# Fused attention and gated FFN on one core: remainder weights as 128-partition loads, narrower first gate/up tiles, and a later place for V

## The chip, the cores and the metric

One Trainium2 chip, one of its cores. The metric is device time in microseconds (us) of one launch. The kernel before took 590.39 us (median of 3 runs, 590.12 to 590.76). A ratio is the mean time of one kernel's runs over that of the other's runs of the same rounds, so it isn't quite the ratio of the medians that stand beside it. Intervals are 95%.

In the profile PE is TensorE, PEld its weight loads, DVE VectorE, ACT ScalarE, POOL GpSimd, SP SyncE. A `q` after an engine's name marks its sequencer, which issues DMAs. A "load" is a DMA from memory to on-chip SBUF.

## The reference, cut to what matters

```python
B, S, D, F = 1, 2048, 576, 4608      # bf16; 32 heads of 18; causal window of 256
xn = layernorm(x)
q, k, v = split(xn @ wqkv)
s = softmax_windowed(q @ k.T * 18**-0.5) @ v @ wo
g = silu((sigmoid(xn @ w_gate) * (xn @ w_up)) @ w_down)
return x + s * g
```

All matrix products contract over D = 576 = 4 x 128 + 64 (or over F = 36 x 128). The 64 rows left over are the *remainder* of a weight matrix.

## The kernel before

TensorE works in pairs of 64-row matmuls: one on partitions 0 to 63, one on 64 to 127, side by side. A gate/up tile is 9 such pairs per 512 tokens. Eight pairs take the wide part of the weights (512 rows on 128 partitions). One pair takes the remainder: gate's 64 rows on the lower partitions, up's on the upper.

```python
ROWS = (slice(0, 64), slice(64, 128))

def pair(eng, outs, lhs, rhs, start, stop, swap=0):        # every matmul comes from here
    for i in range(2):
        t = i ^ swap
        res = eng.matmul(outs[i], lhs(ROWS[t], i), rhs(ROWS[t], i), ..., tile_position=(64 * t, 0))
```

Wide parts come in as one load each. Remainders come in as two loads of 64 partitions each:

```python
def load_nat(self, dst, src, ...):
    return self.dma(dst, src[RD:D, :].rearrange("(k p) c -> p k c", p=P), ...)

def load_rem(self, dst, srcs, ...):                        # RD = 64
    return [self.dma(dst[ROWS[t], :], src[0:RD, :], ...) for t, src in enumerate(srcs)]
```

The order of every engine is fixed when the program is built. A planner with its own estimates of durations places the operations, and `o.slack` makes it believe that a load lands later than it would otherwise assume. Gate/up weights come in groups of two tiles: 256 KB of gate, 256 KB of up, and their remainders (`wgr`), the latter for several groups at once. The first three tiles run in two parts of 256 tokens, because the tokens' normalization and transposes come in block by block (128 tokens a block). While nothing real can run, PE multiplies zeros (warm-up) to hold its clock up.

```python
if c == 0 and wg in REM:                                   # REM = {0: (0, 2, 1), 2: (2, 6, 3), 3: (6, 18, 7)}
    f8 = slice(REM[wg][0] * WG * P, REM[wg][1] * WG * P)
    self.op_wgr[wg] = self.load_rem(self.wgr[:, f8], (self.wg[:, f8], self.wu[:, f8]), ...)
...
for part in range(2):                                      # tiles 0 to 2, 256 tokens a part
    los = [gate_up(ft, hs[ft], 0, None if part else hs[ft], part) for ft in range(early)]
    ...
```

The softmax here doesn't subtract the row's maximum and nothing guards it: scores larger than these inputs give would overflow.

Of the kernel before, what the change touches and what calls it, by code (L numbers as in the profile page):

```python
# [5 lines left out]
ALU = mybir.AluOpType  # L6
# [49 lines left out]
NWARM = 110  # L56
NQK = 5
REM = {0: (0, 2, 1), 2: (2, 6, 3), 3: (6, 18, 7)}
# [5 lines left out]
SHARE_NS = 300.0  # L64
DMA_BYTES_PER_NS = 300.0
# [60 lines left out]
class Pool:  # L126
# [11 lines left out]
    def pick(self, n, barred=()):  # L138
        free = []
        for u in self.units:  # L140
            if u in barred:
                continue
            h = self.last[u]
            if h is None:
                free.append((0.0, u))
            elif h.rel and all(r.idx >= 0 for r in h.rel):
                free.append((max(r.end for r in h.rel) + 90.0, u))
        if len(free) < n:
            return None
        free.sort()  # L150
        got = free[:n]
        return max(t for t, _ in got), sorted(u for _, u in got)
# [70 lines left out]
class Builder:  # L223
# [38 lines left out]
    def alloc_memory(self):  # L262
# [21 lines left out]
        self.wgr, _ = seq("wgr", [P, F])  # L284
# [92 lines left out]
    def load_x(self, c, i=0):  # L377
        if c == 0:
            for i in range(BPC):
                t = self.x0[:, i, :]  # L380
                src = self.x[i * P:(i + 1) * P, :]
                if i == BPC - 1:
                    src = src.rearrange("(a p) d -> a p d", a=8)
                self.x_dma[i] = (self.dma(t, src, P * D * 2, f"dma:x{i}", ("x0", i), prio=0), t)
            return
        st = c * BPC + i
        slots, dd = [], []
        for _ in range(2):
            s_, d_ = self.r_xr.produce()
            slots.append(s_)  # L390
            dd += d_
        assert slots[1] == slots[0] + 1
        o = self.dma(self.xr[:, slots[0]:slots[0] + 2, :],
                     self.x[st * P:(st + 2) * P, :].rearrange("(t p) d -> p t d", p=P),
                     2 * P * D * 2, f"dma:x{st}", ("x", slots[0]), deps=[dd, self.hm[6] if c == 1 else None], prio=5)
        o.slack = 5000.0
        for j in range(2):
            self.x_dma[st + j] = (o, self.xr[:, slots[j], :])
# [5 lines left out]
    def load_rem(self, dst, srcs, name, lane, prio, deps=()):  # L404
        return [self.dma(dst[ROWS[t], :], src[0:RD, :], RD * src.shape[1] * 2, name, lane + (t,), deps=deps, prio=prio)
                for t, src in enumerate(srcs)]

    def build_consts(self):
# [24 lines left out]
        self.op_wqk += self.load_rem(self.wqkr[:, :], (wq, wk), "dma:wqkr", ("wqkr",), 5)  # L433
# [3 lines left out]
        self.op_wv += self.load_rem(self.wvr[:, :], (wv[:, 0:288], wv[:, 288:D]), "dma:wvr", ("wvr",), 6)  # L437
# [7 lines left out]
    def build_attn_consts(self):  # L445
        op = self.op
        d = [self.ln_rs]
        vv = self.v_aug[:, 0:NVS * VSZ].rearrange("p (g d) -> p g d", d=VH)
        o = op("POOL", 400, lambda e: e.memset(vv[:, :, DH:VH], 1.0), "init:vones", deps=d, prio=1)
        self.op_vones = o  # L450
        self.op_vzero = o = op("POOL", 100, lambda e: e.memset(self.v_aug[:, NVS * VSZ:NVS * VSZ + VH], 0.0), "init:vzero", deps=[o], prio=1)
        self.op_qz = o = op("POOL", 4300, lambda e: e.memset(self.qk[:, :, :, :], 0.0), "init:qz", deps=[o], prio=1)
        self.op_kz = o = op("POOL", 2200, lambda e: e.memset(self.kprev[:, :, :], 0.0), "init:kz", deps=[o], prio=1)
        lo = slice(0, SW)
        o = op("POOL", 150, lambda e: e.memset(self.mask[lo, :], 1.0), "init:m0", deps=[o], prio=1)
        o = op("POOL", 200, lambda e: e.affine_select(self.mask[lo, 0:SW], self.mask[lo, 0:SW], pattern=[[-1, SW]],
                                                      compare_op=ALU.is_ge, fill=0.0, base=-1, channel_multiplier=1), "init:m1", deps=[o], prio=1)
        o = op("POOL", 200, lambda e: e.affine_select(self.mask[lo, SW:P], self.mask[lo, SW:P], pattern=[[1, SW]],
                                                      compare_op=ALU.is_ge, fill=0.0, base=0, channel_multiplier=-1), "init:m2", deps=[o], prio=1)
        self.op_mask = op("DVE", 200, lambda e: e.tensor_copy(self.mask[SW:P, :], self.mask[lo, :]), "init:m3", deps=[o], prio=1)  # L460
        hs = []
        for q in range(4):
            for t in range(2):
                hs.append(op("DVE", 60, lambda e, q=q, t=t: e.memset(self.half[32 * q:32 * q + 32, t:t + 1], float(q % 2 == t)),
                             f"init:half{q}{t}", deps=d, prio=1))
        self.op_half = hs

    def build_ln(self, c):
# [3 lines left out]
        for i in range(BPC):  # L472
            st = c * BPC + i
            if c and i % 2 == 0:
                self.load_x(c, i)
            pr = 2 if c or i > 1 else 0
# [18 lines left out]
            dup = op("DVE", 180, lambda e, sn=sn: e.tensor_copy(self.xnr[:, sn, 0:RD], self.xnr[:, sn, RD:2 * RD]),  # L495
                     f"ln:dup:{st}", deps=[ap], prio=pr)
            if c:
                self.r_xr.release(i % 2, ap)
            self.r_st.release(ss, ap)
            if c:  # L500
                fl = self.flip(self.xnT[:, xs, :, i * P:(i + 1) * P], self.xnr[:, sn, :], f"flip:x:{st}", ("fx", xs, i),
                               deps=[dup, war], prio=2)
                self.r_xn.release(sn, fl)
                self.op_xnT[c].append(fl)
                continue
            h = self.pool_s.hold()

            def f_tr(eng, h=h, sn=sn):
                return self.transposes(eng, h, lambda r, o: self.xnr[r, sn, o:o + P])
            tr = op("PE", KB * 29.5, f_tr, f"tr:{st}", deps=[dup, self.op_ident, war], prio=pr if c else 0, acq=h)  # L510
            self.r_xn.release(sn, tr)

            def f_xe(eng, h=h, i=i, xs=xs):
                dst = self.xnT[:, xs, :, i * P:(i + 1) * P].rearrange("p k (t c) -> p t k c", t=2)
                if eng is self.nc.scalar:
                    return eng.activation(dst, self.tr_src(h), ACTF.Copy)
                return eng.tensor_copy(dst, self.tr_src(h))
            dve = st == BPC - 1
            xe = op("DVE" if dve else "ACT", dve_ns(KB * P, 1.9) if dve else act_ns(KB * P), f_xe, f"xe:{st}", deps=[tr], prio=pr)
            h.release(xe)  # L520
            self.op_xnT[c].append(xe)

    def transposes(self, eng, h, src):
        res = None
        for k in range(KB):
            for t in range(2):
                o = h.units[0] * 2048 + t * 1024 + k * 64
# [17 lines left out]
    def build_qk(self, c, gi):  # L545
# [25 lines left out]
        for u in range(H):  # L571
# [12 lines left out]
            for w, (dst, src) in enumerate(moves):  # L584
                o = self.dma(dst, src, n_ * 2 * NT * 2 // len(moves), f"dma:sp:{c}:{u}:{w}:{gi}", ("qk", par, gi),
                             deps=[ev, war, self.op_qz], prio=1, eng="POOL")
                self.op_sp.setdefault((c, hg), []).append(o)
# [18 lines left out]
    def build_v(self, c):  # L606
        op = self.op
        xs = c % 2
        for i in range(BPC):
# [6 lines left out]
                               [self.op_xnT[c][i], self.op_wv, war])  # L616
# [16 lines left out]
    def build_attn(self, c, hg):  # L633
# [128 lines left out]
        if (c, hg) == (0, 0):  # L762
            self.op_wo_w = [self.load_nat(self.wo_sb[:, :, :], self.wo, "dma:wo", ("wo",), 8, [pv])]
            self.op_wo_w += self.load_rem(self.wor[:, :], (self.wo[:, 0:288], self.wo[:, 288:D]), "dma:wor", ("wor",), 8, [pv])
# [39 lines left out]
    def build_ffn(self, c):  # L804
# [16 lines left out]
        def weights(wg):  # L821
# [5 lines left out]
            if c == 0 and wg in REM:  # L827
                f8 = slice(REM[wg][0] * WG * P, REM[wg][1] * WG * P)
                self.op_wgr[wg] = self.load_rem(self.wgr[:, f8], (self.wg[:, f8], self.wu[:, f8]), f"dma:wgr:{wg}", ("wgr", wg), REM[wg][2])
            if c == 0:  # L830
                ds += self.op_wgr[0 if wg < 2 else 2 if wg < 6 else 3]
# [13 lines left out]
        def gate_up(ft, h, half, acq, part=None, deps=()):  # L845
            sw, fc = slots[ft // WG], slice((ft % WG) * P, (ft % WG + 1) * P)
            n = NT if part is None else NT // 2
            t0 = n * (part or 0)
            xin = self.op_xnT[c] if part is None else self.op_xnT[c][2 * part:2 * part + 2]

            def lhs(r, t, k):
                return self.wgs[r, sw, k - 1, t, fc] if k else self.wgr[r, ft * P:(ft + 1) * P]

            def f(eng):
                return turn(eng, [bank(h, w)[:, t0:t0 + n] for w in range(2)], lhs, lambda r, t, k: x_in[r, k, t0:t0 + n], half)
# [18 lines left out]
        if early:  # L874
# [3 lines left out]
            for part in range(2):  # L878
                los = [gate_up(ft, hs[ft], 0, None if part else hs[ft], part) for ft in range(early)]
                for ft in range(early):  # L880
                    u = gate_up(ft, hs[ft], 1, None, part, [los[ft]])
                    if part:
                        tail(ft, hs[ft], u)
                    if part and ft == 1:
# [103 lines left out]
    def schedule(self):  # L988
# [12 lines left out]
        nsched = 0  # L1001
        while nsched < len(ops):
            best = None
            for e in ENGS:
# [9 lines left out]
                for o in cand:  # L1014
                    st = max(free[e], ready_t[o.cidx])
                    units = None
                    if o.acq is not None:
# [6 lines left out]
                        got = mine.pick(o.acq.n, barred)  # L1024
# [14 lines left out]
            _, o, stt, units = best[1]  # L1039
            if o.eng == "PE":  # L1040
# [145 lines left out]
```

## Time and profile before

| what | before |
|---|---|
| time, span of the profiled run | 590.39 us, 587.1 us |
| PE busy | 571.6 us, 97% of the span |
| PE's longest wait | 4.72 us at 24.17, for V's remainder |
| clock at half | from 22.2 to 29.0 us, by the clock record of the trace |
| first gate/up matmul; end of tile 2 | 9.49 us; 14.78 + 1.47 = 16.25 us |
| PE idle: to 25 us / 25 to 580 / after | 7.4 / 3.4 / 4.7 us |

The table is read from the stretches and the timeline: idle is the length of a stretch less PE's busy time in it. PE is busy nearly all the time, so the change can only win from the first 30 us (idle and half clock) and from the 3.4 us in the middle. The prediction below shows the lines for this.

### The profile page before, as it was taken

The numbers are of one execution on the slowest core, as the hardware profiler recorded it, in microseconds if no ns is written. First come the engines' busy times: TensorE is split into PE (matmuls) and PEld (weight loads), VectorE is DVE, ScalarE is ACT, GpSimd is POOL, SyncE is SP. The second block draws the span as 40 slices with busy tenths as digits, with TensorE's granted clock in tenths as the row PEclk, the third lists the DMA queues.
The fourth block names the chain that finished last, engine by engine and source line by source line (L and its number), as shares of the span: only waits on it lengthen the run. The fifth ranks groups of instructions, "written<-read, shape, count | busy, mean of one in ns | idle before, by whom it ended". The sixth has DMA issues, their size and how long they took to land.

```text
span 587.1 us, 21476 instructions
## 1 busy us (share of the span) xinstructions
PE 571.6 (97%) x9552; PEld 361.9 (62%) x9552; DVE 347.8 (59%) x841; ACT 266.5 (45%) x379; POOL 175.3 (30%) x286
## 2 busy tenths in 40 slices
PE   8699999999999999999999999999999999999996
PEld 7454545588975556555687775555457764444786
DVE  4347789855879976477778477877331133333123
ACT  2226566622638573656773557584220022323111
POOL 5333646305557533026445343620000000000000
PEclk9799999999999999999999999999999999999999
DMA  8949666462303442323621112523450114542010
GB/s 231 261 116 247 188 161 190 137 157 61 92 20 105 128 115 74 106 76 111 132 34 48 33 31 84 149 85 108 142 145 12 34 58 121 152 144 73 2 42 22
DMA packets 103948, 62.05 MB, mean 106 GB/s; under 512 B 15116, under 2 KB 102236, under 8 KB 103856
## 3 DMA queue, kind: packets, MB, share of 16 engines
q1 hardware_dynamic: 98736, 55.95, 35.1%
q0 software_dynamic: 5120, 4.74, 3.2%
q8 instruction: 75, 1.23, 0.9%
q14 instruction: 17, 0.14, 0.1%
HBM read 51.61 MB, written 2.36 MB: 92 GB/s over the span
## 4 chain that ended last, share of the span: by engine, by line
PE 88%; DVE 3%; DMA 3%; SPq 3%; POOL 1%; issue 1%; ACT 1%; DVEq 0%
PE ps L96 87%; SPq L252 3%; DMA qk<-qd 2%; POOL qk L252 1%; DMA wvr<-in_A_wqkv_dram 1%; DVE qd L567 1%; DVE hT L866 1%; DVE pvs L745 1%; ACT tring L863 1%; PE ps L529 0%; DVE s_attn L969 0%; DVE expr L692 0%; DVE thf L974 0%; DVE o_tok L757 0%; DVE kx L644 0%
## 5 line engine op out<-in xcount | busy, mean ns | idle before, releaser
L96 PE MATMUL ps<-xnT,wgs 64*128 64x512 bf16 (+1 forms) x2352 | 287.3, 372 | 0.0
L96 PEld LDWEIGHTS ps<-xnT,wgs 64*128 64x128 bf16 x2352 | 112.1, 94 | 113.6 <-PE ps L96 1.4
L679 ACT ACTIVATE expr<-ps 128x1024 bf16<-128x1024 f32 (+2 forms) x160 | 153.1, 984 | 44.9 <-PE ps L96 44.2
L96 PE MATMUL ps<-wd_sb,hT 64*128 64x288 bf16 (+2 forms) x2448 | 156.2, 276 | 0.0
L863 ACT ACTIVATE tring<-ps 128x512 bf16<-128x512 f32 x144 | 85.9, 598 | 136.5 <-PE ps L96 135.0
L866 DVE SCALAR_TENSOR_TENSOR hT<-tring,ps 128x512 bf16<-128x512 bf16 x144 | 98.6, 686 | 82.0 <-ACT tring L863 79.8
L96 PEld LDWEIGHTS ps<-wd_sb,hT 64*128 64x128 bf16 x2448 | 115.7, 94 | 24.8
L252 POOL DMA_DIRECT2D qk<-qd x160 | 81.8, 521 | 71.8 <-DVE qd L567 61.0
L644 POOL TENSOR_SCALAR kx<-kprev,small 128x256 bf16<-128x256 bf16 x64 | 63.0, 991 | 97.9 <-PE ps L96 97.8
L692 DVE TENSOR_TENSOR expr<-expr,mask 128x256 bf16<-128x256 bf16 (+2 forms) x232 | 66.9, 311 | 25.3 <-ACT expr L679 23.5
L96 PE MATMUL ps<-qk,kx 64*128 64x320 bf16 (+4 forms) x736 | 58.1, 251 | 2.1 <-DMA qk<-qd 0.9
L745 DVE TENSOR_REDUCE pvs<-ps 64x304 f32<-64x608 f32 x64 | 50.4, 788 | 15.5 <-PE ps L96 14.3
L96 PE MATMUL ps<-xnT,wgr 64*128 64x512 bf16 (+1 forms) x294 | 55.4, 372 | 2.4 <-DMA wgr<-in_B_w_up_dram 1.2
L96 PEld LDWEIGHTS ps<-qk,kx 64*128 64x128 bf16 x736 | 31.3, 94 | 27.6 <-DVE qd L567 1.6
L959 ACT ACTIVATE thf<-ps 128x576 bf16<-128x576 f32 (+3 forms) x22 | 11.4, 520 | 75.4 <-PE ps L96 74.9
L96 PEld LDWEIGHTS ps<-v_aug,expr 64*128 64x128 bf16 x2432 | 35.4, 93 | 5.4 <-DVE expr L692 0.2
L96 PE MATMUL ps<-v_aug,expr 64*128 64x19 bf16 (+1 forms) x2432 | 35.8, 170 | 0.0
L96 PE MATMUL ps<-xnT,wqk 64*128 64x512 bf16 x256 | 32.7, 376 | 0.0
L644 DVE TENSOR_SCALAR kx<-qk,small 128x512 bf16<-128x512 bf16 x64 | 23.8, 396 | 10.3 <-DMA qk<-qd 8.5
L567 DVE CAST qd<-ps 128x1024 bf16<-128x1024 f32 (+1 forms) x20 | 22.2, 1116 | 8.2 <-PE ps L96 8.0
L962 DVE SCALAR_TENSOR_TENSOR thf<-thf,ps 128x576 bf16<-128x576 bf16 x12 | 9.0, 752 | 29.6 <-ACT thf L959 29.4
L96 PEld LDWEIGHTS ps<-xnT,wgr 64*128 64x128 bf16 x294 | 14.6, 94 | 16.0 <-issue 2.7
(65 smaller groups left out, 295.9 us busy)
## 6 DMA issues: line engine op xcount, KB each, us to landing
wgs<-in_B_w_gate_dram SPq DMA_DIRECT2D x72, 256.0 KB, 3.1
wgs<-in_B_w_up_dram SPq DMA_DIRECT2D x72, 256.0 KB, 3.5
wd_sb<-in_B_w_down_dram SPq DMA_DIRECT2D x9, 576.0 KB, 5.0
qk<-qd POOLq DMA_DIRECT2D x100, 36.0 KB, 2.0
xf<-in_A_x_dram SPq DMA_DIRECT2D x16, 144.0 KB, 2.7
out_dram<-xf SPq DMA_DIRECT2D x16, 144.0 KB, 1.8
xr<-in_A_x_dram SPq DMA_DIRECT2D x6, 288.0 KB, 3.5
wqk<-in_A_wqkv_dram SPq DMA_DIRECT2D x2, 576.0 KB, 7.1
```

The source lines that it names most:

```text
L96: res = eng.matmul(outs[i], lhs(ROWS[t], i), rhs(ROWS[t], i), start=start, stop=stop, tile_position=(64 * t, 0))
L252: o = self.op(eng, DMA_ISSUE_NS[eng], lambda e: e.dma_start(dst, src), name, deps, prio, nbytes=nbytes)
L567: return eng.tensor_copy(dst, self.both(h, n))
L644: return e.tensor_scalar(self.kx[:, sx, pos:pos + n_ // SW, t, :], src.rearrange("p (s k) -> p s k", k=SW), self.half[:, t:t + 1], None, A ...
L679: return eng.activation(self.expr[:, se, :, lo * SW:NT], self.both(h, NT)[:, :, lo * SW:NT], ACTF.Exp, scale=SM_SCALE)
L692: return eng.tensor_tensor(e_, e_, m_, ALU.mult)
L745: return eng.tensor_reduce(out[ROWS[i]], src, mybir.AxisListType.X, ALU.add)
L863: th = op("ACT", act_ns(NT), lambda e: e.activation(self.tring[:, st, :], bank(h, 0), ACTF.Tanh, scale=0.5), f"th:{c}:{ft}", deps=[pg, dt_ ...
L866: mu = op("DVE", dve_ns(NT), lambda e: e.scalar_tensor_tensor(self.hT[:, ft, :], self.tring[:, st, :], 1.0, bank(h, 1), ALU.add, ALU.mult) ...
L959: return e.activation(v2(t)[:, a:b, :], y2()[:, a:b, :], ACTF.Tanh, scale=0.25)
L962: q1 = op("DVE", dve_ns(w), lambda e: e.scalar_tensor_tensor(v2(t), v2(t), 1.0, y2(), ALU.add, ALU.mult), f"fq1:{nm}", deps=[th, f2], prio=0)
```

## The change

Its intent is to keep PE fed in the first 30 us.

1. *Remainders on 128 partitions.* Two 64-row blocks go in one load to all 128 partitions. A group's gate remainder needs a partner, so gate of an even group travels with gate of the next, up of an odd group with up of the next; every other group then has gate and up mirrored between the partition halves (`flip`). ACT issues the first two, SP the rest.
2. *First tiles* in three parts, of 128, 128 and 256 tokens.
3. *V later*: 5 us of slack on V's loads.
4. *Blocks 2 and 3* come in one load, are transposed into one PSUM buffer, and leave it by ACT and DVE, half each. POOL computes the duplicated 64 columns.
5. *Planning*: 1 us slack on the q/k moves, scores at least 0.8 us apart, and another choice among free PSUM buffers. Set-up fills and the normalization of blocks 1 to 3 get later priorities.

The core of the diff (cuts marked by `...`):

```diff
+PARTS = ((0, 1), (1, 2), (2, 4))
-REM = {0: (0, 2, 1), 2: (2, 6, 3), 3: (6, 18, 7)}
+SPACE_NS = 800.0
...
-    def load_rem(self, dst, srcs, name, lane, prio, deps=()):
-        return [self.dma(dst[ROWS[t], :], src[0:RD, :], RD * src.shape[1] * 2, name, lane + (t,), deps=deps, prio=prio)
-                for t, src in enumerate(srcs)]
+    def load_rem(self, dst, src, step, n, name, lane, prio, deps=()):
+        a = src[0:RD, 0:n]
+        return self.dma(dst, bass.AP(a.tensor, a.offset, [(step, 2), a.ap[0], (1, n)]), P * n * 2, name, lane, deps=deps, prio=prio)
...
+        for o in self.op_wv:
+            o.slack = 5000.0
...
+                    if wg % 2 == i and wg < NFT // WG - 1:
+                        a = w[0:RD, wg * nw:(wg + 1) * nw]
+                        src = bass.AP(a.tensor, a.offset, [(nw, 2), a.ap[0], (1, nw)])
+                        j = (wg + i) * P
+                        self.op_wgr.setdefault(wg, []).append(self.dma(
+                            self.wgr[:, i, j:j + nw], src, P * nw * 2, f"dma:wgr:{wg}", ("wgr", wg % NWS, i), prio=pr,
+                            deps=[dw, None if wg else self.op_tab], eng="SP" if wg else "ACT"))
...
-            for part in range(2):
+            for part in range(len(PARTS)):
```

## The prediction

> **What bounds the kernel now.** I read the engine rows, the slices, the waits, then one table of stretches and the timeline of the first 30 us. The first says TensorE:
>
> ```profile
> span 587.1 us, 21476 instructions
> ...
> PE 571.6 (97%) x9552; PEld 361.9 (62%) x9552; DVE 347.8 (59%) x841; ACT 266.5 (45%) x379; POOL 175.3 (30%) x286
> ...
> PEclk9799999999999999999999999999999999999999
> DMA  8949666462303442323621112523450114542010
> ```
>
> PE is busy 97% of the span, so only time in which PE idles, runs throwaway work or runs at a low clock can be won. The slices show the place: the second slice (14.7 to 29.4 us) is the only one with a granted clock below 9 tenths, and the DMA engines are at their fullest there. The waits of PE name it:
>
> ```profile
> PE ps L96 <- DMA wvr<-in_A_wqkv_dram: 4.7, 1, 4.7
> PE ps L96 <- DMA wgr<-in_B_w_up_dram: 1.2, 1, 1.2
> PE ps L96 <- DVE hT L866: 1.1, 5, 0.3
> PE ps L96 <- DVE hT L419: 1.1, 1, 1.1
> PE ps L96 <- DMA qk<-qd: 0.9, 1, 0.9
> ```
>
> The reader sees two waits for remainder weights (the 64 rows that 576 leaves over 4 times 128): 4.7 us for V's, 1.2 us for the first gate/up tile's. Nothing else is over about a microsecond. By stretches of 1 us (columns: busy PE, weight loads, DVE, ACT, POOL, then clock, DMA share, GB/s):
>
> ```profile
> 18.00:19.00 1.00, 1.00 (x12) 0.48 (x10) 0.00 (x0) 0.00 (x0) 1.00 (x3) 1.00 1.09 274
> 19.00:20.00 1.00, 0.45 (x6) 0.00 (x0) 0.00 (x0) 0.51 (x1) 0.88 (x1) 1.00 1.15 297
> 20.00:21.00 1.00, 0.00 (x0) 0.00 (x0) 0.43 (x3) 0.09 (x1) 0.00 (x0) 1.00 1.18 199
> ...
> 23.00:24.00 1.00, 0.00 (x0) 0.00 (x0) 0.00 (x0) 0.00 (x0) 0.00 (x0) 0.50 1.07 201
> 24.00:25.00 1.00, 0.83 (x8) 0.67 (x10) 0.00 (x0) 0.00 (x0) 0.00 (x0) 0.50 1.17 160
> ...
> 28.00:29.00 1.00, 1.00 (x10) 0.62 (x8) 0.94 (x3) 0.86 (x3) 0.00 (x0) 0.50 0.99 310
> ```
>
> PE stops at 19.45, starts at 24.17, and then runs at half clock until about 29. While PE waits, the DMA engines are full but move only about 200 GB/s. The timeline gives the start and the stall:
>
> ```profile
> 7.39 0.91 PE L96 MATMUL ps<-hT 64*128 64x128 bf16 x26
> 9.49 0.29 PE L96 MATMUL ps<-xnT,wgr 64*128 64x256 bf16 x2 [1.19 <-DMA wgr<-in_B_w_up_dram]
> 14.78 1.47 PE L96 MATMUL ps<-xnT,wgs 64*128 64x256 bf16 x24
> 18.64 0.81 PE L96 MATMUL ps<-xnT,wgs 64*128 64x512 bf16 x6
> 24.17 0.42 PE L96 MATMUL ps<-wvr,xnT 64*128 64x288 bf16 x2 [4.72 <-DMA wvr<-in_A_wqkv_dram]
> 28.44 1.33 PE L96 MATMUL ps<-xnT,wgs 64*128 64x512 bf16 x8
> ```
>
> All PE work before 9.49 is warm-up on zeros or transposes. So up to 24.17 PE does only tiles 0 to 2 (six half-tiles of about 1.0 us, 5.9 us), tiles 3 and 4 (1.95 us each; 8 pairs take 1.72 us start to start at 42.81 to 44.53 in the longer timeline, 9 pairs 1.95) and four transposes: about 10.4 us of useful work in 24.17 us.
>
> **What the Trainium skill says.** (1) "TensorE: Matmul & The Clock Gate", Part 1 on the HAM clock gate: after an idle window of about 3.4 us the clock drops to half and returns after about as long busy. The trace agrees: after 4.72 us idle it reads 0.50 until about 29; the shorter 1.19 us idle leaves it at 1.00. (2) "SBUF — State Buffer", "Door 1: The DMA port swizzle": partitions 0 to 63 reach 8 of 16 ports, and two transfers for the two halves don't make up for it. The rates agree in sign: about 200 GB/s at 20 to 24 us, where the queue holds mostly 64-partition remainders, against 338 GB/s at 14 to 16 us with the wide 128-partition loads. The page's cause isn't isolated by this. (3) "DMA: Bandwidth & Descriptors", "Queues, rings and completion order": ACT and SP have rings of their own, between which each DMA engine takes turns. A small load put on ACT's ring need not stand behind all that SP queued. The trace before has no ACT DMA. (4) Same page, "Why a DMA increments its semaphore by 16 and not by 1": a load runs on as many engines as divide both sides' outer dimensions, so x block 3, cut in 8, should use 8 engines. The trace does not show this.
>
> **Part by part.**
>
> *Remainders on 128 partitions.* Six gate/up remainder loads on 64 partitions become one load per pair of groups with gate (even groups) or up (odd) of both. The mirroring only swaps which row half holds gate and up; pairs and sizes stay: PE cost 0. Queued ahead of V's remainder before: x 576, four groups of 512, gate/up remainders 128 + 256, wqk 1152, wqkr 144, wv 576, wvr 72, in all 4952 KB. Gate/up remainders for groups 0 to 3 are now 96 + 64 + 64 + 64 = 288 KB, so 96 KB less; at some 290 GB/s 0.35 us. wgr, wqkr and wvr together are some 500 KB; at 300 instead of 200 GB/s I estimate 0.8 us saved. The 768 KB burst behind wvr, which shares the engines while it drains, goes away: perhaps 1 us. V's weights then land near 21.7 us instead of 24.0.
>
> *V later in PE's order.* PE's order is fixed when the program is built. Five microseconds of slack are added to V's loads in the builder's plan, so more tiles are placed before V. I use that plan for order only. Before it placed two tiles (3 and 4) before V; 5 us hold 2.5 more, so about five (3 to 7). Their weights, groups 1 to 3, landed by 15.7 us already (issue at 10.55 plus 5.1). From the end of tile 2 near 15 us, five tiles of 1.95 end at 24.7, later than the 21.7 at which V's weights land. So the 4.72 us wait is filled with work that had to be done anyway, and the clock never drops. The half clock cost: 24.17 to 28.44 is 4.27 us for work that takes half at full clock, 2.1 lost, plus about 0.1 after. Gain 4.7 + 2.2 = 6.9 us; I keep back 0.5 us for a small wait.
>
> *First tiles by 128, 128, 256 tokens.* They can start on block 0 alone. Before, its eviction ends at 7.10 (6.40 + 0.70). The change removes block 1's statistics from block 0's path (0.45) and moves the copy for the remainder rows to POOL beside the main one (0.18 + gaps), so about 6.7. Gate and up of group 0 landed at 5.9 and 6.8 (2.66 + 3.2, 3.14 + 3.7), the remainders only at 9.4 (4.30 + 5.1). With ACT issuing the latter from about 2.3 us they should be there by 7. So PE starts near 7.2 instead of 9.49. But tile 2 needs group 1, which landed at 11.1 (5.56 + 5.5); one issue earlier and a lighter queue give perhaps 9.8. Tiles 0 and 1 on one block are 18 pairs of about 60 ns (26 matmuls, so 13 pairs, of 128 columns take 0.91 us with the pipeline's tail): 1.1 us. PE then waits from 8.3 to 9.8. Remaining work from there: tile 2's 0.55, second part 1.65, third 2.95, so the end is near 15.1 with a few tenths of transposes, against 16.25. Cost of the narrow tiles: 54 pairs of 60 instead of 27 of 112 ns, +0.2, contained in this. Gain about 1.0 us.
>
> *Blocks 2 and 3 together.* Ten transposes each into one buffer, then ACT and DVE take half each, 0.70 and 0.49 us side by side, instead of a 0.70 at 11.38 and a 0.49 at 12.59 in turn. Both are ready by about 11.5, before the third part wants them near 12. It avoids a wait, worth nothing by itself.
>
> *Planning changes.* Scores at least 0.8 us apart, the lower-numbered free PSUM buffer first, 1 us slack on the q/k moves. They reorder the same instructions. PE idle is 15.5 us of the span; 7.4 is before 24.17 (sum of the stretches) and 4.7 after 580, so only 3.4 lies in between. I count 0.6 of the 3.4 as saved (the 0.9 us q/k wait is the candidate).
>
> Sum: 6.9 - 0.5 + 1.0 + 0.6 = 8.0 us. 590.4 - 8.0 = **582.4 us**, 1.4% faster.
>
> **Rivals.** *A: the start is bound by bytes, and the wait only moves.* For it: DMA share is 1.0 to 1.18 from 5 to 28 us, and V's weights stay last. Against it: PE has 9.7 us of other work whose weights are ahead in the queue. If the plan places only three tiles before V, or V's weights stay at 24, about 2 us idle stays, below what dropped the clock: time 584 to 586. *B: the early start is worth nothing, because group 1's weights gate tile 2.* If they stay at 11.1, PE waits longer after 8.3 and tile 2 ends no sooner: the 1.0 goes, time 583.5. *C: the reordering costs.* A gap rule for scores can leave ACT's exponentials late, and new waits of some tenths over 32 head groups would make 3 to 5 us: 586 to 587. Against it: PE has filler through 100 to 400 us (idle only 1.0 us there), and ACT is 45% busy. *D: the plan fits so well that the idle time in between goes too:* another 2 to 3 us, 579.5 to 580.
>
> **Range and chances.** Gain over 2% means below 578.6, 11.8 us: it would need the whole stall and clock loss (6.9), over 2 us at the start and all of the 3.4 between. I give 0.05. Slower by 2% needs over 11.8 us of new waits; the change adds no work: 0.01. A, B and C pull up, D down: 8 in 10 from 579.5 to 586.0.
>
> **What would show it.** Right: first gate/up matmul near 7 us at 64x128; a wait of 1 to 2 us for group 1 soon after; no wait on V's remainder over 1 us, clock 1.00 from 15 to 30 us; five full tiles before V; PE idle between 25 and 580 us of 2 to 4 us; V's start still near 24 us. Wrong: V waits over 3 us again, with the clock at 0.5 after it (fill failed); or tile 2 finishing after 16 us (start failed); or more than 5 us of PE idle in the middle (reordering costs).

## The result, and the profile after

| | before | after |
|---|---|---|
| median (range) | 590.25 us (588.0 to 590.76, 4 runs) | 585.96 us (585.74 to 586.45, 4 runs) |
| ratio | | 0.9936 [0.9909, 0.9962] |
| span of the profiled run | 587.1 us | 584.2 us |

The kernel got 0.64% faster where 1.35% was forecast: less than half of the gain came. The engine rows and slices of the kernel after:

```profile
span 584.2 us, 21509 instructions
...
PE 571.1 (98%) x9560; PEld 356.9 (61%) x9560; DVE 345.1 (59%) x837; ACT 267.8 (46%) x379; POOL 177.9 (30%) x290
...
PEclk8899999999999999999999999999999999999999
DMA  6687796843314333342501114433340114542010
```

PE's work is the same (571.1 against 571.6 us busy). The clock dip moved: before it was in the second slice alone, now it reads 8 in the first as well. And the DMA row opens 6, 6 where before it opened 8, 9: the DMA engines are *less* busy in the first two slices, 29 us. PE's waits, and the timeline of the start (start, duration, engine, line, what; in brackets the wait before it and what ended it):

```profile
PE ps L97 <- DMA wgr<-in_B_w_up_dram: 3.7, 2, 2.5
...
PE ps L97 <- ACT v_aug L651: 0.9, 1, 0.9
```

```profile
5.33 3.05 SPq L253 DMA_DIRECT2D wgs<-in_B_w_gate_dram  x1
...
9.52 0.23 PE L97 MATMUL ps<-xnT,wgr 64*128 64x128 bf16 x2 [2.52 <-DMA wgr<-in_B_w_up_dram]
...
12.02 0.29 PE L97 MATMUL ps<-xnT,wgr 64*128 64x128 bf16 x2 [1.17 <-DMA wgr<-in_B_w_up_dram]
...
19.11 1.47 PE L97 MATMUL ps<-xnT,wgs 64*128 64x256 bf16 x24
...
29.56 0.29 PE L97 MATMUL ps<-wvr,xnT 64*128 64x288 bf16 x2
```

The wait for V is gone from the list: V's remainder matmuls at 29.56 have no bracket. The two waits for gate/up remainders, 1.2 us in all before, are now 3.7 us. The first gate/up matmul starts at 9.52 (9.49 before), and tile 2 ends at 19.11 + 1.47 = 20.58 us (16.25 before). So the start *lost* 4.3 us, and that came off what V won. The stretches from 8 to 16 and from 10 to 15 us (busy PE, weight loads, DVE, ACT, POOL, then clock, DMA share, GB/s), before:

```profile
8.00:16.00 8.00, 6.66 (x140) 5.77 (x133) 2.64 (x15) 1.75 (x4) 7.71 (x8) 1.00 0.98 281
...
10.00:15.00 5.00, 4.85 (x103) 4.23 (x100) 0.76 (x3) 0.82 (x2) 4.88 (x3) 1.00 0.94 257
```

and after:

```profile
8.00:16.00 8.00, 5.25 (x128) 4.87 (x130) 1.14 (x11) 0.70 (x1) 6.48 (x7) 0.71 0.60 165
...
10.00:15.00 5.00, 3.77 (x94) 3.35 (x90) 0.63 (x9) 0.70 (x1) 4.30 (x4) 0.64 0.68 195
```

PE waits for loads while the DMA engines are busy 60% of the time and move 165 GB/s, where before they were full and moved 281. By the clock record of the trace, half clock now lasts from 11.4 to 18.2 us: 6.8 us as before, in another place.

The chain that ended last shows the wait for a remainder as one piece (start, duration, what). After:

```profile
4.43 7.45 DMA wgr<-in_B_w_up_dram
```

That is group 1's remainder: 64 KB, issued at 4.43 us, landed at 11.88. Why does it take 7.45 us when the DMA engines aren't full? The packets of the queues answer (packets, MB, share of 16 engines). After:

```profile
q1 hardware_dynamic: 100310, 55.85, 34.9%
...
q10 hardware_dynamic: 210, 0.10, 0.1%
```

`q10` is ACT's queue. It carries two loads only: a new two-block gate remainder (64 KB) and a half up remainder (32 KB). In rows of 512 bytes that is 192 data packets. The trace has 18 packets of four bytes beside them, which are the completion writes, one for each engine that a load uses. The half load, 64 rows outermost, accounts for 16. So the two-block load, whose source pattern `[(step, 2), 64 rows, n columns]` has an outermost dimension of size 2, used **2 of 16 engines**. That is a count of packets and not yet a proof that it costs anything; the experiments are for that.

### The profile page after: what moved, and what is told of

The parts are those of the page before. It is cut to its first block, busy times and chain, and to the rows that moved or that the text cites. A ratio compares the mean times of both kernels' runs of the same rounds, so it can differ in the third digit from the quotient of the medians.

```text
span 584.2 us, 21509 instructions
## 1 busy us (share of the span) xinstructions
PE 571.1 (98%) x9560; PEld 356.9 (61%) x9560; DVE 345.1 (59%) x837; ACT 267.8 (46%) x379; POOL 177.9 (30%) x290
## 4 chain that ended last, share of the span: by engine, by line
PE 94%; DVE 2%; DMA 1%; issue 1%; ACT 1%; SPq 1%; DVEq 0%
PE ps L97 94%; DMA wgr<-in_B_w_up_dram 1%; DVE hT L908 1%; SPq L253 1%; PE ps L553 0%; ACT tring L905 0%; ACT expr L704 0%; DVE s_attn L1012 0%; DVE thf L1017 0%; DVE xf L1022 0%; DVE expr L717 0%; ACT v_aug L651 0%; DVE kx L669 0%; DVE wq L446 0%; DVEq L1162 0%
## 5 line engine op out<-in xcount | busy, mean ns | idle before, releaser
L97 PE MATMUL ps<-xnT,wgs 64*128 64x512 bf16 (+2 forms) x2400 | 291.9, 371 | 0.3
L704 ACT ACTIVATE expr<-ps 128x1024 bf16<-128x1024 f32 (+2 forms) x160 | 156.5, 983 | 68.9 <-PE ps L97 68.2
L97 PEld LDWEIGHTS ps<-wd_sb,hT 64*128 64x128 bf16 x2448 | 113.8, 94 | 27.4
L97 PE MATMUL ps<-xnT,wgr 64*128 64x512 bf16 (+2 forms) x300 | 56.4, 372 | 5.2 <-DMA wgr<-in_B_w_up_dram 3.7
L97 PE MATMUL ps<-qk,kx 64*128 64x320 bf16 (+4 forms) x736 | 59.6, 251 | 0.0
L1002 ACT ACTIVATE thf<-ps 128x576 bf16<-128x576 f32 (+3 forms) x22 | 11.4, 519 | 71.9 <-PE ps L97 70.9
L97 PEld LDWEIGHTS ps<-xnT,wgr 64*128 64x128 bf16 x300 | 15.0, 95 | 18.2 <-issue 4.5
```

The source lines that it names most:

```text
L704: return eng.activation(self.expr[:, se, :, lo * SW:NT], self.both(h, NT)[:, :, lo * SW:NT], ACTF.Exp, scale=SM_SCALE)
L1002: return e.activation(v2(t)[:, a:b, :], y2()[:, a:b, :], ACTF.Tanh, scale=0.25)
```

## The experiments

*Theory.* The new two-block loads, 20 in all, run on 2 engines each. So a load of 64 KB puts 32 KB on each of two engines instead of 4 KB on each of 16, the early weights land late, and that gives back about half of the gain. *Rivals.* The idle time and half clock of the start are to blame by themselves; V's slack does nearly everything; ACT's separate queue is at fault; the early burst of loads is; B of the prediction (group 1's weights gate tile 2 in any case); C (the planning rules cost).

Twelve kernels ran, four to a call, all correct, each in up to five rounds. The medians of the kernel before were 589.27, 587.88 and 589.01 us in the three calls (11 runs each).

| run | call | median (range), us | ratio to before |
|---|---|---|---|
| x_k16 | 1 | 580.64 (580.12 to 581.63) | 0.9854 [0.9841, 0.9867] |
| x_vslack | 1 | 586.21 (585.38 to 588.27) | 0.9955 [0.9939, 0.9970] |
| x_remonly | 1 | 598.04 (595.94 to 602.82) | 1.0160 [1.0128, 1.0191] |
| x_warm | 1 | 585.77 (585.51 to 587.39) | 0.9952 [0.9938, 0.9966] |
| x_vsp | 2 | 587.12 (583.99 to 589.01) | 0.9978 [0.9953, 1.0004] |
| x_p2 | 2 | 580.05 (579.77 to 580.43) | 0.9862 [0.9841, 0.9884] |
| x_early | 2 | 581.27 (580.86 to 582.29) | 0.9888 [0.9870, 0.9905] |
| x_noplan | 2 | 581.15 (580.14 to 583.10) | 0.9884 [0.9866, 0.9903] |
| x_k16wgr | 3 | 581.32 (580.91 to 581.68) | 0.9862 [0.9842, 0.9882] |
| x_k16rem | 3 | 584.54 (584.16 to 585.40) | 0.9919 [0.9901, 0.9938] |
| x_norem | 3 | 580.84 (580.79 to 581.79) | 0.9858 [0.9837, 0.9879] |
| x_best | 3 | 582.91 (582.03 to 583.36) | 0.9887 [0.9866, 0.9908] |

### x_k16: the same kernel, each two-block load as two 64-partition loads in its place

```diff
+        o.fn = lambda e: [e.dma_start(dst[ROWS[t]], parts[t]) for t in range(2)]
+        o.nd = 2                    # the semaphore counts 32 for the two together
```

The planner sees one load as before, so the order on PE, ACT, DVE and POOL is that of the change.

> The changed kernel with the same order on every compute engine, but each two-block remainder load issued as two loads of 64 partitions. Theory E (the two-block loads have an outermost dimension of 2, so each runs on 2 of the 16 DMA engines, arrives late and holds up SP's queue): first gate/up matmul at 7.0 to 8.0 us instead of 9.5, SP's 3.05 us issue at 5.3 us shrinks below 1.5 us, clock 1.00 from 10 to 20 us, tile 2 done near 15.5 us instead of 20.6, time near 581.5 to 583. Rival R (the queue of ACT is slow for its first loads, or the start is bound by bytes): first matmul still after 9 us, clock 0.5 again, time 585 to 587.

580.64 us, 0.9854. The interval lies clear of the change's [0.9909, 0.9962]: with the same bytes, the same order and *more* DMA instructions, the two-engine loads cost 0.9936 - 0.9854 = 0.82% of 589 us, 4.8 us. ACT's queue and the early burst of bytes are here as in the change, so neither of these two rivals explains the loss. The queue rows of this kernel:

```profile
q1 hardware_dynamic: 100880, 55.85, 34.8%
...
q10 hardware_dynamic: 240, 0.10, 0.1%
```

On ACT's queue 240 = 192 + 48: three loads of 16 engines each. On SP's queue there are 570 packets more than in the change for the same megabytes: 570 = 19 x (32 - 2), for the 19 two-block loads that SP issues (16 gate/up, q/k, V, output), each now with 16 + 16 completions instead of 2. The count of engines is settled to the packet. Its stretch from 8 to 16 us:

```profile
8.00:16.00 8.00, 6.63 (x168) 6.08 (x170) 1.65 (x12) 1.41 (x2) 6.49 (x7) 0.79 0.97 260
```

SP's issue, the first gate/up matmul and the last matmuls of tile 2:

```profile
6.19 0.59 SPq L254 DMA_DIRECT2D wgs<-in_B_w_gate_dram  x1
...
8.95 0.29 PE L97 MATMUL ps<-xnT,wgr 64*128 64x128 bf16 x2 [1.90 <-DMA wgr<-in_B_w_up_dram]
...
16.09 1.47 PE L97 MATMUL ps<-xnT,wgs 64*128 64x256 bf16 x24
```

The DMA engines are full again (0.97 against 0.60), and the issue that took SP 3.05 us takes 0.59. But the start isn't yet what was predicted, nor what I expected of this run (7.0 to 8.0 us and 15.5 us): the first gate/up matmul comes at 8.95 us after a wait of 1.90 us, the clock is 0.79 here, and tile 2 ends at 16.09 + 1.47 = 17.56 us.

### x_remonly: the kernel before with the remainder part alone

```diff
-REM = {0: (0, 2, 1), 2: (2, 6, 3), 3: (6, 18, 7)}
-        self.wgr, _ = seq("wgr", [P, F])
+        self.wgr, _ = seq("wgr", [P, 2, F // 2 + WG * P])
+            flip = ft // WG % 2
 # and load_rem, its calls and the loads of wgr as in the change; nothing else of it
```

> The kernel before with the remainder part alone: two-block loads, mirrored odd groups, first group's remainder from ACT's queue. Theory E: the loads on two engines cost; first matmul at 9 to 10 us as before, V's weights later than 24 us, V's wait longer than 4.7 us, time 590.5 to 593. Rival R (128 partitions load faster, as the change intends): V's wait shrinks to 3 us or less, time 588 or less.

598.04 us, 1.6% *slower* than before, worse than expected. PE's timeline shows V's wait, which is 4.72 us in the kernel before:

```profile
27.35 0.42 PE L95 MATMUL ps<-wvr,xnT 64*128 64x288 bf16 x2 [8.39 <-DMA wvr<-in_A_wqkv_dram]
```

Taken alone, the part that the prediction credited with 0.8 us of faster loads lengthens V's wait by 3.7 us. PE stands still from 19 to 27 us with the DMA share at 0.50 from 20 to 25 us. The rest of the 9 us is more half clock (0.50 from 25 to 30 us) and new waits: PE waited 2.4 us on issue and 1.7 us on DVE for expr, where the kernel before has 0.4 us of the first and none of the second at the head of its list. In the full change V's slack hides V's wait, so only the start shows the damage. Here the start hardly suffers: the first gate/up matmul comes at 9.02 us, PE has group 1's remainder at 11.61, and tile 2, in parts of 256 tokens, ends at 16.62 us (16.25 before). Which late load hurts thus depends on what PE's order needs first.

### x_warm: the change with 39 more warm-up pairs before the first tile

```diff
-                return pair(eng, self.halves(h, P), lambda r, t: zero[r, :], lambda r, t: zero[r, :], True, True)
+                return [pair(eng, self.halves(h, P), lambda r, t: zero[r, :], lambda r, t: zero[r, :], True, True)
+                        for _ in range(4 if i >= 41 else 1)][-1]
```

This separates the clock from the loads: more throwaway work fills the first wait.

> The changed kernel with 39 more pairs of warm-up matmuls on zeros before its first tile, some 2.4 us. It adds no useful work and takes no wait away. Theory: the waits at 7.0 to 9.5 us let the clock drop, and the half clock from 11.4 to 18.2 us is about 3 us of the loss; with the clock at 1.00 tile 2 is done near 17.5 us instead of 20.6 and the time is 582.5 to 583.5. Rival (the tiles between 12 and 20 us are held by their loads, not by the clock): clock 1.00 but new waits on loads, time 585 to 586.

585.77 us: no different from the change (0.9952 against 0.9936). The clock did stay up, and tile 2 ended 2.3 us sooner:

```profile
16.77 1.56 PE L97 MATMUL ps<-xnT,wgs 64*128 64x256 bf16 x24
...
24.37 0.39 PE L97 MATMUL ps<-xnT,wqkr 64*128 64x512 bf16 x2 [1.94 <-DMA wqkr<-in_A_wqkv_dram]
```

Then PE ran into the next late two-block load, `wqkr`, waited 1.94 us, and its clock read 0.67 from 25 to 30 us. That profiled run took 587.39 us; the four fastest of the six runs, 585.51 to 585.83 us, list a mean clock of 1.00, and one run of the change itself does too, at 585.74 us against 585.88 to 586.45 for the three others. So the half clock isn't what holds the time; the late loads are.

### x_k16wgr and x_k16rem: which of the two-block loads

x_k16wgr splits only the gate/up remainders, x_k16rem only those of q/k, V and output.

```diff
 # x_k16wgr: in weights() alone
-                        src = bass.AP(a.tensor, a.offset, [(nw, 2), a.ap[0], (1, nw)])
+                        src = [w[0:RD, (wg + t) * nw:(wg + t + 1) * nw] for t in range(2)]
 # x_k16rem: in load_rem alone
-        return self.dma(dst, bass.AP(a.tensor, a.offset, [(step, 2), a.ap[0], (1, n)]), P * n * 2, ...)
+        return self.halves_dma(dst, [src[0:RD, t * step:t * step + n] for t in range(2)], P * n * 2, ...)
```

> The changed kernel in the same order, with only the gate/up remainders split into pairs of 64 partitions; the q/k, V and output remainders stay two-block loads. Theory E: the start is cured (no wait of over 1.5 us for group 1's remainder, tile 2 done near 17 to 18 us), but the q/k remainder, 144 KB on two engines, now makes PE wait 2 to 5 us near 21 us: time 583 to 585. Rival (the gate/up loads are all of it): 580 to 581.5.

> The reverse: the changed kernel in the same order, with only the q/k, V and output remainders split; the gate/up remainders stay two-block loads. Theory E: the start is as slow as in the changed kernel (first matmul near 9.5 us, tile 2 done after 19.5 us) and most of the loss stays: 584 to 586. Rival (the larger q/k and V loads are all of it): 580 to 582.

581.32 and 584.54 us. The packets on SP's queue rise by 480 = 16 x 30 and by 90 = 3 x 30. With the gate/up loads split nearly everything is won back; the expected wait for `wqkr` was only 0.51 us, so my expectation for x_k16wgr missed and its rival, that gate/up loads are nearly all of it, holds. With the others split the start stays as slow as in the change. From x_k16rem, the stretch and the chain:

```profile
8.00:16.00 8.00, 5.36 (x130) 4.98 (x132) 1.21 (x12) 0.81 (x2) 6.55 (x7) 0.68 0.62 167
```

```profile
4.43 7.34 DMA wgr<-in_B_w_up_dram
```

Group 1's remainder takes 7.34 us to land and the DMA share is 0.62, as in the change. In this order, what comes early does the harm.

### x_norem: the change with its remainder part undone

The old layout, the old two loads per remainder issued by SP, no mirroring; the rest of the change stays.

```diff
+REM = {0: (0, 2, 1), 2: (2, 6, 3), 3: (6, 18, 7)}
-        self.wgr, _ = seq("wgr", [P, 2, F // 2 + WG * P])
+        self.wgr, _ = seq("wgr", [P, F])
-            flip = ft // WG % 2
 # and load_rem, its calls and the loads of wgr as before
```

> The changed kernel with the remainder part undone: loads, layout and issuing queue as before, all else as changed. Theory: better than the changed kernel, since no load runs on two engines, but worse than the split pairs, since the 768 KB burst on 64 partitions again stands in the queue at 18 to 28 us: time 581 to 584. Rival (gathering the remainders is worth something even on two engines): 586 or more.

580.84 us, 0.9858: the change without its first part gains what was forecast for the whole. Its start:

```profile
7.83 0.23 PE L98 MATMUL ps<-xnT,wgr 64*128 64x128 bf16 x2 [0.16 <-DMA wgr<-in_B_w_up_dram]
...
9.93 0.23 PE L98 MATMUL ps<-xnT,wgr 64*128 64x128 bf16 x2 [0.91 <-DMA wgs<-in_B_w_up_dram]
...
14.20 1.47 PE L98 MATMUL ps<-xnT,wgs 64*128 64x256 bf16 x24
```

This is the picture that the prediction drew: first tile at 7.83 (predicted 7.2), then a wait for group 1's weights (0.91 us; predicted 1.5), tile 2 done at 15.67 (predicted 15.1), V's first matmul at 25.22 without a wait (predicted 24.7), clock 1.00. It also takes away the thought that the old burst of remainders, 768 KB behind V's, is a cost: with it the time is that of x_k16.

### x_vslack and x_vsp: V's slack on the kernel before

```diff
+        for o in self.op_wv:
+            o.slack = 5000.0
```

> The kernel before with nothing changed but 5 us of planning slack on V's loads. Theory: filling V's wait is the one part that gains; no V wait over 1 us, clock 1.00 from 20 to 30 us, 6 to 7 us gained, time 583.5 to 584.5, so this alone beats the whole change. Rival (the wait only moves, the bytes are late for the next tiles as well): time 588 or more.

586.21 us, 0.9955. V's wait went and the clock stayed at 1.00, but only 0.45% was won; I had expected about 1%. Two new waits took its place:

```profile
20.48 0.39 PE L96 MATMUL ps<-xnT,wqkr 64*128 64x512 bf16 x2 [0.93 <-DMA wqkr<-in_A_wqkv_dram]
...
34.98 0.35 DVE L646 TENSOR_SCALAR kx<-qk,small 128x512 bf16<-128x512 bf16 x1 [4.23 <-DMA qk<-qd]
...
36.88 0.39 PE L96 MATMUL ps<-xnT,wqkr 64*128 64x512 bf16 x2 [2.96 <-DVE v_aug L629]
```

VectorE stands 4.23 us on a q/k move that its fixed order puts ahead of V's evictions, and PE, which needs the PSUM behind those, waits 2.96 us. The two new waits of PE, 3.9 us, are about what is missing from the expected gain. The change's 1 us of slack on the q/k moves looked like the remedy for this, so I tried it on top (x_vsp):

```diff
+                o.slack = 1000.0                     # on each q/k move
```

> The kernel before with two planning changes only: 5 us slack on V's loads and 1 us slack on the q/k moves. With V's slack alone PE got a new wait of 2.96 us near 34 us, because VectorE stood 4.23 us before a q/k move with two V evictions behind it in its order. Theory: the q/k slack puts those evictions first; that wait goes and the time falls by some 3 us to 582.5 to 584. Rival (V's eviction waits for something else, or the wait moves elsewhere): 585.5 to 587 as with V's slack alone.

587.12 us, 0.9978 [0.9953, 1.0004]: no gain, and that theory fell. In the profiled run the wait at 37 us shrank to 1.57 us, but `wqkr` took 1.78 us and a wait for pvs 1.53 us more; the runs spread over 5 us (583.99 to 589.01). Why they spread so is open. What stands is that filling V's wait alone isn't worth the 6.4 us that I gave it. In x_norem, which has the old loads but all of the rest, the gain is there in full.

### x_p2, x_early, x_noplan: the smaller parts, each on x_k16

```diff
-PARTS = ((0, 1), (1, 2), (2, 4))                    # x_p2
+PARTS = ((0, 2), (2, 4))
-deps=[dw, None if wg else self.op_tab]              # x_early: ACT issues the first remainders before its table load
+deps=[dw]
-SPACE_NS = 800.0                                    # x_noplan, with the old choice of a free PSUM buffer
+SPACE_NS = 0.0
```

> The changed kernel with remainder loads as pairs of 64 partitions, and the first three tiles in two parts of 256 tokens instead of 128, 128, 256. Theory P (the small parts cost more than they gain, because the first tile's weights land only near 9 us and the gap before lets the clock drop): tile 2 done near 15.5 to 16.5 us instead of 17.6, clock 1.00 to 20 us, time 579 to 580. Rival (the small parts gain the 1 us that the prediction gave them): 581.5 to 582.

> The changed kernel with remainder loads as pairs of 64 partitions, and ACT issues the first group's remainders before its table load, near 0.9 instead of 2.3 us. Theory (the first tile waits for these small loads, which stand among the big ones): first gate/up matmul near 7.5 us instead of 8.95, no clock loss, 1 to 2 us gained, time 578.5 to 580. Rival (the first tile then waits for group 0's main weights, or the start is held by group 1 anyway): first matmul near 7.5 to 8.5, tile 2 no earlier, 580 to 581.

> The changed kernel with remainder loads as pairs of 64 partitions, without the 0.8 us rule for scores and with the old choice of PSUM buffer; the slacks stay. Theory (these two reorder the same work and save little): 580 to 582. Rival (they carry a real part of the gain in the attention stretch): 583 to 585, with more PE idle between 60 and 400 us than the 1.6 us with them.

x_p2, 580.05 us: with the old two parts of 256 tokens the time is that of x_k16 (0.9862 and 0.9854, intervals overlap), and tile 2 ends at 15.91 us. With x_k16's loads the narrow first tiles are worth nothing that these runs show; with the old loads (x_norem) they weren't undone. x_early, 581.27 us: the first tile comes 1.2 us sooner than in x_k16 and then waits for group 1:

```profile
7.79 0.23 PE L97 MATMUL ps<-xnT,wgr 64*128 64x128 bf16 x2 [0.58 <-issue]
...
10.58 0.23 PE L97 MATMUL ps<-xnT,wgr 64*128 64x128 bf16 x2 [1.46 <-DMA wgr<-in_B_w_up_dram]
```

That is rival B: an early start is spent waiting for group 1, and the time doesn't improve (0.9888 against 0.9854, if anything slower; x_k16 ran in another call). x_noplan, 581.15 us: 0.9884 against x_k16's 0.9854 with overlapping intervals. The planning rules are worth some 0.3% by these figures, which they can't tell from nothing; PE's idle time between 60 and 400 us doesn't grow without them (1.2 us against 1.6).

### x_best: an attempt at a better version

x_p2 with x_early's edit, and x blocks 2 and 3 loaded behind group 0.

```diff
-                         ("x0", 2), prio=0)
+                         ("x0", 2), prio=2)
```

> Remainder loads as pairs of 64 partitions, first three tiles in two parts of 256, ACT issues the first remainders before its table load, and x blocks 2 and 3 are loaded behind group 0's weights. Theory: each moves the start, which is held by arriving bytes: first tile near 8.0 instead of 8.8 us, tile 2 done near 15.3 us instead of 15.9: 578.5 to 580, the fastest of all. Rival (group 1's weights or blocks 2 and 3 hold the start anyway): 580 to 581.

582.91 us, 0.9887: not better. The later blocks made PE's transposes wait 1.7 us, and tile 2 ended at 16.99 us. The best are x_p2, x_k16 and x_norem, at 580.05 to 580.84 us; nothing here tells them apart.

## Why the prediction was right or wrong

**Failed: "Remainders on 128 partitions".** It said of the new loads "at 300 instead of 200 GB/s I estimate 0.8 us saved", and of the first ones, "with ACT issuing the latter from about 2.3 us they should be there by 7". PE got group 0's at 9.52 and group 1's at 12.02, DMA throughput fell from 281 to 165 GB/s between 8 and 16 us, the part costs about 9 us taken alone (x_remonly), and running its loads on 2 engines costs 4.8 us inside the change (x_k16). I took the wider destination for a faster load, by the half-of-the-ports point of the skill, and never looked at how many engines the new pattern can use. The rule was on my own table: I cited it as point (4), but applied it only to old block 3, cut in 8. Even there the trace can be asked: SP's queue has 98736 packets before and 98720 in x_norem, where blocks 2 and 3 share one load, and the data packets are equal in number; and before, the four x loads, first on the queue, have 64 = 4 x 16 four-byte packets ahead of the first weights'. So block 3 ran on 16 engines and not on 8. Its eight pieces lie one behind another in memory; whether its pattern was joined into one on the way isn't shown. In the Trainium skill, "DMA: Bandwidth & Descriptors", section "Rules for kernel authors", the row "Use all 16 engines" says it outright: an outermost dimension below 16 confines the load to at most that many engines. For `[(step, 2), 64 rows, n]` that is 2. The trace agrees for these loads, by 18 completion writes on ACT's queue and 19 x 30 packets on SP's. (Of point (2), "two transfers" stands in the section "Can I just issue two DMAs to hit both halves?" of "SBUF — State Buffer", not under "Door 1".)

Not all of the late start is this: in x_k16, with every remainder load on 16 engines, group 0's last remainder still came at 8.95 us, so "by 7" was too early by itself. Most of the loss lies behind the first tile: from its start to the end of tile 2 it took 11.06 us in the change, 8.61 in x_k16 and 7.84 in x_norem. Two slips hardly bear on it: the three savings add up to 2.15 us, so V's weights would land at 21.85 and not 21.7 us, and PE ran 14 pairs before V, not the 18 of two tiles; the other four stand at 28.44.

**"V later in PE's order": right in the change, wrong about its cause.** The wait and its half clock went, as predicted. From the end of tile 2 to V PE had 9.0 us of work (20.58 to 29.56), where I had counted five tiles, 9.75 us; only the first 4.1 us were tiles, then came 4.2 us of q/k projections. But V's slack alone brings 0.45% on the kernel before (x_vslack), where the plan's order makes new waits of 0.93 and 2.96 us. The 6.4 us therefore belong to parts 2 to 5 together, and which of them completes it is not shown; x_vsp says it isn't the q/k slack alone.

**"First tiles by 128, 128, 256": wrong in the change, overrated without its fault.** In the change tile 2 ended 4.3 us later instead of 1.0 sooner. With the loads mended by x_norem it ended 0.6 us sooner than before, and x_p2, without narrow tiles, is as fast. Rival B was right in x_early; that the 0.6 us reached the total isn't shown.

**"Blocks 2 and 3", "planning changes".** Middle idle (25 us to PE's last matmul before the tail) fell from 3.4 to 2.8 us in the change, the 0.6 predicted; it is 1.7 us in x_k16 and 3.0 in x_norem, so the match is partly luck. Rival C, reordering that costs, didn't appear.

**Rivals A and the sum.** A, "the start is bound by bytes, and the wait only moves", had the right outcome with the wrong reason: the wait moved, but to loads that left DMA engines idle. That the measured time falls into its 584 to 586 us is luck. The predicted sum, 8.0 us, is met by the change without its flaw (0.9854 and 0.9858 are 8.6 and 8.4 us of 589); x_norem meets it without any of the first part's savings, which the sum counted only as V's weights landing sooner. Of my tests, "tile 2 finishing after 16 us (start failed)" is the one that fired.

**Open.** No record here names the engines, so whether all 20 loads share the *same* two is not shown. Nor is it shown why x_k16's first tile still comes 1.1 us later than x_norem's: the last remainder that it needs takes 5.3 us to land from ACT's queue (issued at 3.54), against 3.8 us from SP's in x_norem (issued at 3.85). A two-block load on all 128 partitions *and* 16 engines wasn't tried: the pattern would need its rows outermost on both sides, which this placement of the blocks doesn't give.

## What to carry to other kernels

Before reshaping a load, look at the outermost size of the pattern as it is handed to the DMA, not at the number of partitions that it ends on; then count the completion packets in the trace, which gave the number of engines here to the packet. A wait for a load while the DMA share is well under 1 (0.60 here) is a reason to ask for few engines before too many bytes. And when several parts of a change go in together, run it once with each suspicious part undone: the whole gained 0.6%, and it gains 1.4% without its first part.

## What the Trainium skill lacked or had wrong

- "DMA: Bandwidth & Descriptors", "Rules for kernel authors": the row "Two transfers to disjoint partition halves" advises against them and for one 128-partition transfer. Here two halves beat one 128-partition load of two blocks, 580.64 against 585.96 us. The row "Use all 16 engines" further down is the one that decides; the first doesn't refer to it. "SBUF — State Buffer", "Can I just issue two DMAs to hit both halves?", has the same gap: "one transfer spanning all 128 partitions" can still run on 2 engines.
- No page tells to count a queue's four-byte packets to learn how many engines a load ran on. Here they show it: 2 for a two-block load, 16 for a half, and 570 = 19 x 30 more when 19 loads are split.
- No page tells what a load on 2 engines does to the loads behind it. Here an SP issue took 3.05 us at 5.33 us (0.59 in x_k16), and the DMA share fell from 0.98 to 0.60 between 8 and 16 us.
- "DMA: Bandwidth & Descriptors", "Queues, rings and completion order": rings of ACT and SP take turns on each engine. It gives no time for a small load beside a full ring; I inferred that one on ACT's ring would overtake. The 32 KB up remainder on it took 5.3 us to land even in x_k16, where every remainder load uses 16 engines (5.9 us in the change).
- "TensorE: Matmul & The Clock Gate", "Part 1: The HAM clock gate": it speaks of an idle window of about 3.4 us, and not of how much work a window may hold and still count as idle. In the change the clock fell at 11.4 us with no single wait over 2.52 us; PE was busy 1.33 us of the 3.41 us before. In the kernel before it fell at 22.2 us, 2.75 us after PE had stopped at 19.45; PE was busy 0.66 us of the 3.41 us before.
